# Two of three short DFTs on TensorE with 64-row tiles instead of 32-row tiles

## The chip, the cores and the metric

One core of one Trainium2 chip. The metric is the device time of one execution in microseconds (us). Executions of one kernel differ by up to about 1 us here, so medians are quoted, and every timed kernel was run in turn with the kernel before on the same chip. A ratio below is the mean time of one kernel's runs over that of the other's of the same rounds, so it is not quite the ratio of the medians.

TensorE is written PE, VectorE DVE, ScalarE ACT, GpSimd POOL, as the profile does. PEld is PE's weight loads. "Granted clock" is the share of PE's full clock that the profile records: 0.50 or 1.00 in the fast runs here.

## The reference, cut to what matters

```python
P = jnp.exp(logdA[:, :, None] * l[None, None, :])
K = jnp.einsum("dn,dnl,dn->dl", Cc, P, dB).real      # one kernel K per channel d
Kf = rfft(pad(K)); Uf = rfft(pad(u))
y  = irfft(Uf * Kf)[:L]                              # long convolution
h  = x + y + u * Dskip
out = h + SwiGLU(layernorm(h))
```

There are 640 channels and 2048 tokens. Only the transform of K (`Kf` above) is changed. The kernel works on blocks of 256 tokens, so the transform of K is a DFT over 256 positions, l = 16 j + i, and it is done in three chunks of 256, 256 and 128 channels.

## The kernel before: the parts that matter

`k_mm` leaves K in PSUM with 128 partitions that are 4 pairs of channels x 16 values of j x 2 channels of the pair. `k_evac` copies it to SBUF as `kc` and multiplies with a mask that keeps the row's own channel of the pair. `k_dft` contracts over the partitions with the DFT table `wt`, in four 32-row tiles, each into a part of PSUM of its own. Their matmuls overlap in the trace: in chunk 2 one starts every 8.1 ns, and each is shown as about 0.19 us long. For each of 16 values of i and 4 parts f of the output there are 4 loads and 4 matmuls: 256 of each per chunk.

```python
def k_evac(h, pk, kc, b):
    ...
    for c2 in range(2):
        src = pk[...].rearrange("p h (g x c) -> p x h g c", g=gh, c=2)[:, :, :, :, c2]
        dst = ...
        S.mul(out=dst, in_=src, mul=mask[:, c2:c2 + 1])      # 128 x 512

def k_dft(h, kc, mid=None):
    cg, nu = CHUNKS[h] // 8, 4 // CUT[h]
    pp = [ps2("g"), ps2("g")]
    for i in range(II):                                       # 16
        if mid and i == II // 2:
            mid()
        for f in range(NFT):                                  # 4
            for blk in range(4):
                T.matmul(pp[blk // 2][:, blk % 2, f * 2 * cg:(f + 1) * 2 * cg],
                         lhsT=wt[32 * blk:32 * blk + 32, i, f * P:(f + 1) * P],
                         rhs=kc[32 * blk:32 * blk + 32, (i * nu + blk % nu) * 2 * cg: ...],
                         ..., tile_position=(32 * blk, 0))
    return pp
```

`rhs` has 64 columns in chunks 0 and 1 and 32 in chunk 2. `kf_evac` then copies the result into `kf` on ScalarE, and the convolution's product (`z`, line 586) reads `kf` on VectorE. The stretch of the schedule around chunk 2 that the argument turns on, in program order:

```python
for b in range(n_mm(2)):
    k_evac(2, k_mm(2, at2, bt2, b), kc, b)
run(p0, 1)
stats(1)                                   # 1/sqrt(var): 3 steps on DVE, 8 on POOL
kr_mul(SPLIT[0], (0,))                     # ACT
inv(0, SPLIT[0])                           # PE, ACT
ln1(1)                                     # DVE: normalise, needs stats(1)
h_add(0, SPLIT[0], (0,))                   # DVE
pb = k_dft(2, kc, lambda: [fwd(0, SPLIT[1], part) for part in range(2)])
kr_mul(SPLIT[0], (1,))                     # ACT
kf_evac(2, pb, "SSSS")                     # ACT, copies of kf
...
run(p0)                                    # DVE: product with kf of chunk 2
```

Of the kernel before, what the change touches and what calls it, by code (L numbers as in the profile page):

```python
# [8 lines left out]
F32 = mybir.dt.float32  # L9
I32 = mybir.dt.int32  # L10
ACT = mybir.ActivationFunctionType
ALU = mybir.AluOpType

TB = 256
NFT = 4
JJ = 16
II = 16
EPS = 1e-5
CHUNKS = [256, 256, 128]
CUT = [4, 2, 2]  # L20
# [3 lines left out]
def mkap(t, offset, dims):  # L24
    return bass.AP(tensor=t.tensor, offset=t.offset + offset, ap=[list(d) for d in dims])

@with_exitstack
def kernel(
    ctx: ExitStack,
    tc: tile.TileContext, A_u, A_A_re, A_A_im, A_B_re, A_B_im,  # L30
         A_C_re, A_C_im, A_log_dt, A_Dskip, B_x, B_w1, B_w3, B_w2, out, dbg=None):
    nc = tc.nc
    P = nc.NUM_PARTITIONS
# [9 lines left out]
    V, S, T, G = nc.vector, nc.scalar, nc.tensor, nc.gpsimd  # L43
    CWM = 3 * max(CHUNKS) // 2
    d0s = [sum(CHUNKS[:h]) for h in range(len(CHUNKS))]
# [3 lines left out]
    def ps2(tag="d", dt=F32):  # L49
        return ps.tile([P, 2, 512 if dt == F32 else 1024], dt, name="ps2", tag=tag, bufs=2)  # L50

    dram = ctx.enter_context(tc.tile_pool(name="dram", bufs=1, space=bass.MemoryType.DRAM))
    keep = ctx.enter_context(tc.tile_pool(name="keep", bufs=1, side="left"))
# [4 lines left out]
    early = ectx.enter_context(tc.tile_pool(name="early", bufs=1, side="right"))  # L58
# [38 lines left out]
    toki = early.tile([P, 2], I32, name="toki")  # L97
# [7 lines left out]
    V.tensor_copy(out=tokf[:], in_=toki[:])  # L105
    parity = early.tile([P, 1], I32, name="parity")
    V.tensor_single_scalar(out=parity[:], in_=toki[:, 0:1], scalar=1, op=ALU.bitwise_and)
    mask = keep.tile([P, 2], F32, name="mask")
    sil = keep.tile([P, 1], F32, name="sil")
    V.tensor_scalar(out=mask[:, 0:1], in0=parity[:], scalar1=-1.0 / TB, scalar2=1.0 / TB, op0=ALU.mult, op1=ALU.add)  # L110
    V.tensor_scalar(out=mask[:, 1:2], in0=parity[:], scalar1=1.0 / TB, scalar2=None, op0=ALU.mult)
    angs = []

    def angle(kt):
# [19 lines left out]
    wt = kp.tile([P, II, NFT * P], BF16, name="wt")  # L134
# [177 lines left out]
    def k_mm(h, at, bt, b):  # L312
        nt, cg = CUT[h], CHUNKS[h] // 8
        gw, gh = 3 * cg // 2, min(4 * nt, cg // 2)
        m, n = P // nt, 8 // nt
        pk = ps2()

        def mm(half, gi, part, n1, first, last):
            g = (cg + gh * b + gi) if n1 else (half * (cg // 2) + gh * b + gi)
            r = slice(64 * half, 64 * half + 64) if n1 else slice(0, P)  # L320
            for t in range(nt):
                c = (part * gw + g) * P
                T.matmul(pk[m * t:m * t + m, half, gi * m:gi * m + m].rearrange("p (i c) -> p i c", c=n),  # L323
                         lhsT=at[r, c + m * t:c + m * t + m],
                         rhs=bt[r, c:c + P].rearrange("p (i m) -> p i m", m=8)[:, :, n * t:n * t + n],
                         start=first, stop=last, tile_position=(r.start, m * t), skip_group_check=True)

        for half in range(2):
            for gi in range(gh):
                for part in range(2):  # L330
                    mm(half, gi, part, False, gi == 0 and part == 0, False)
        for gi in range(gh):
            for part in range(2):
                for half in range(2):
                    mm(half, gi, part, True, False, gi == gh - 1 and part == 1)
        return pk
# [4 lines left out]
    def k_evac(h, pk, kc, b):  # L341
        nt, cg = CUT[h], CHUNKS[h] // 8
        gh, nu = min(4 * nt, cg // 2), 4 // nt
        for c2 in range(2):
            src = pk[:, :, 0:P // nt * gh].rearrange("p h (g x c) -> p x h g c", g=gh, c=2)[:, :, :, :, c2]
            dst = mkap(kc[:], c2 + 2 * gh * b, [[kc[:].ap[0][0], P], [2 * cg, II * nu], [cg, 2], [2, gh]])
            S.mul(out=dst, in_=src, mul=mask[:, c2:c2 + 1])  # L347

    def k_dft(h, kc, mid=None):
        cg, nu = CHUNKS[h] // 8, 4 // CUT[h]  # L350
        pp = [ps2("g"), ps2("g")]
        for i in range(II):
            if mid and i == II // 2:
                mid()
            for f in range(NFT):
                for blk in range(4):
                    T.matmul(pp[blk // 2][:, blk % 2, f * 2 * cg:(f + 1) * 2 * cg], lhsT=wt[32 * blk:32 * blk + 32, i, f * P:(f + 1) * P],  # L357
                             rhs=kc[32 * blk:32 * blk + 32, (i * nu + blk % nu) * 2 * cg:(i * nu + blk % nu + 1) * 2 * cg], start=(i == 0 and f == 0), stop=(i == II - 1 and f == NFT - 1),
                             tile_position=(32 * blk, 0), skip_group_check=True)
        return pp  # L360

    def kf_evac(h, pp, engs):
        cg, d0 = CHUNKS[h] // 8, d0s[h]
        for k in range(2):
            for f2 in range(2):
                src = pp[k][:, :, 0:NFT * 2 * cg].rearrange("p b (f g c) -> p f g b c", f=NFT, c=2)[:, 2 * f2:2 * f2 + 2]
                dst = mkap(kf[:], f2 * 2 * D + d0 + 4 * k, [[kf[:].ap[0][0], P], [D, 2], [8, cg], [2, 2], [1, 2]])
                if engs[2 * k + f2] == "S":
                    S.copy(out=dst, in_=src)
                else:  # L370
                    V.tensor_copy(out=dst, in_=src)
# [157 lines left out]
    kc = kp.tile([P, II * 4 * (max(CHUNKS) // 8)], BF16, name="kc", bufs=1)  # L529
    pk = k_mm(0, at0, bt0, 0)  # L530
    stg = [b_rest(1, bt1, "sin", ig) for ig in IGS]
    k_evac(0, pk, kc, 0)
    at2 = kp.tile([P, 2 * JJ * CWM], BF16, name="at", bufs=1)
    S.copy(out=a_view(2, at2)[:, :, :, 0, :], in_=wl2[:].rearrange("p a (q c) -> p a q c", c=2))
    z_mul(1, zs1, ze1)
    run(a_chain(1, at1, zs1))
    pb = k_dft(0, kc)
    for ig, st in zip(IGS, stg):
        b_mul(1, bt1, "sin", ig, st)
    zs2 = z_sin(2)  # L540
    bt2 = b_tile(2)
    b_first(2, bt2, "sin", 1, 8)
    kf_evac(0, pb, "SSSS")
    b_first(2, bt2, "sin", 8, II)
    for k in range(2):
# [9 lines left out]
    kc = kp.tile([P, II * 4 * (max(CHUNKS) // 8)], BF16, name="kc", bufs=1)  # L555
    for b in range(n_mm(1)):
        k_evac(1, k_mm(1, at1, bt1, b), kc, b)
        if b == 0:
            sums(1, 0)
# [5 lines left out]
    for ig, st in zip(IGS, stg):  # L565
        b_mul(2, bt2, "exp", ig, st)
    pb = k_dft(1, kc)
    for part in range(2):
        fwd(0, SPLIT[0], part)
    kf_evac(1, pb, "SSSS")  # L570
    skip(0, ulns[0])
    kc = kp.tile([P, II * 4 * (max(CHUNKS) // 8)], BF16, name="kc", bufs=1)
# [60 lines left out]
    def kr_mul(r, parts=(0, 1)):  # L633
        for part in parts:
            for e in range(2):
                S.mul(out=kr[:, part, e, r], in_=kf[:, 1 - part, e, r], mul=(1.0 if part == e else -1.0))
# [5 lines left out]
    for b in range(n_mm(2)):  # L642
        k_evac(2, k_mm(2, at2, bt2, b), kc, b)
# [4 lines left out]
    ln1(1)  # L648
    h_add(0, SPLIT[0], (0,))
    pb = k_dft(2, kc, lambda: [fwd(0, SPLIT[1], part) for part in range(2)])  # L650
    kr_mul(SPLIT[0], (1,))
    kf_evac(2, pb, "SSSS")
    kctx.close()
    if dbg and "kf" in dbg:
# [76 lines left out]
    for part in range(2):  # L731
        fwd(1, HALVES[1], part)
    kr_mul(SPLIT[1])
    S.activation(out=sil[:], in_=mask[:, 0:1], func=ACT.Silu)
    idle = xs[:, 12:14, 0:256].rearrange("p a (b c) -> p a b c", b=1)
    warm(7, idle)
    h_add(0, SPLIT[1])
# [111 lines left out]
```

## Time and profile before

| | |
|---|---|
| median, 20 runs | 293.88 us (293.34 to 294.40) |
| the profiled run | 294.6 us, span 292.6 us |
| first gate/up matmul of SwiGLU | 112.2 us |
| from there to the end | 180.35 us, PE almost without a break |

The span has two halves. After about 112 us PE works without a break on SwiGLU; before, ACT and DVE are the busy engines and PE waits. So a change in the K-DFT can help only by letting the first gate/up matmul start earlier.

The chain of waits of the kernel before, from 96 to 113 us (start in us, duration in us, what), shows where that start comes from:

```profile
96.59 1.05 PE ps_2186 L604 x2
97.64 0.14 PE ps_2205 L357 x2
...
98.46 0.34 issue
98.81 0.20 PE ps_2205 L357
...
100.30 1.05 ACT kr L636 x2
101.35 2.07 issue
103.42 0.61 ACT kf L369 x3
104.04 0.02 issue
104.06 0.43 DVE z L586
```

L357 is the K-DFT of chunk 2. "issue" is time for which the profile shows nothing that was waited for; the one of 2.07 us stands before the copies of kf, which wait for the K-DFT. The timeline of PE's loads in that K-DFT (start us, duration us, engine, line, operation, shape, count, and in brackets the idle time before) shows what PE did meanwhile:

```profile
97.56 0.80 PEld L357 LDWEIGHTS <-wt 32*128 32x128 bf16 x89 [0.84 <-issue]
98.80 0.38 PEld L357 LDWEIGHTS <-wt 32*128 32x128 bf16 x39 [0.44 <-issue]
99.76 0.76 PEld L357 LDWEIGHTS <-wt 32*128 32x128 bf16 x85 [0.20 <-issue]
102.80 0.41 PEld L357 LDWEIGHTS <-wt 32*128 32x128 bf16 x43 [2.28 <-issue]
```

PE loaded 89 tables and stopped, then 39 and 85 (the transform `mid` sits between), and stopped again for over 2 us, with operands ready (the last copy into `kc` ended at 97.32 us) and 43 pairs of load and matmul to go. From the first gap to the second there are 39 + 85 such pairs and the 8 instructions of `mid`: 2 x 124 + 8 = 256 instructions. The trace has 11 stops of this kind, and from one to the next lie 254 to 256 recorded loads and matmuls, once 512 (3351 loads and 3349 matmuls are recorded, so a few records are missing). On VectorE the stop is a wait of 1.18 us (timeline of DVE, same columns):

```profile
102.19 0.69 DVE L622 BATCH_NORM_STATS2 hst<-xs 128x6 f32<-128x512 bf16 x1
104.06 0.43 DVE L586 TENSOR_TENSOR z<-vt,kf 128x512 bf16<-128x512 bf16 x1 [1.18 <-ACT kf L369]
```

And the queue that fetches instructions, from the page's list of DMA queues (packets, MB, share of 16 engines' span):

```profile
q8 instruction: 26, 0.43, 0.6%
```

0.43 MB in 26 packets is 16 KB each. The 6700 recorded loads and matmuls of PE make 258 per packet, so I take a packet for a block of 256 PE instructions, 64 bytes each (an estimate from these counts).

### The profile page before, as it was taken

What the parts mean: (1) busy time and instruction counts of PE and PEld (TensorE: products, weight loads), DVE (VectorE), ACT (ScalarE), POOL (GpSimd) and SP (SyncE); (2) the same over time, 40 slices, a digit from 0 to 9 for tenths busy, and PEclk for the clock granted to TensorE, in tenths of its full rate; (3) what the DMA queues carried; (4) which work ended last, traced back from release to release, by engine and by line L of the source; (5) the groups of instructions that cost most, each with busy time, mean ns of one, the idle gap of its engine ahead of it and who ended that gap; (6) DMA issues with size and microseconds to landing.
All of it is one profiled execution on the core that took longest, in us unless ns stands there. A gap on an engine that the chain in (4) does not pass through costs nothing.

```text
span 292.6 us, 8071 instructions
## 1 busy us (share of the span) xinstructions
PE 230.3 (79%) x3349; PEld 181.2 (62%) x3351; DVE 230.0 (79%) x512; ACT 210.7 (72%) x450; POOL 53.0 (18%) x171
## 2 busy tenths in 40 slices
PE   3541174234854689999999999999999999999995
PEld 1320133131743437867887887887887887887883
DVE  6799999999899678979949949949959958932111
ACT  3999999999988678867676677677574574553440
POOL 4000100000422203536322322322320020020000
PEclk9999987557565559999999999999999999999999
DMA  5741840000000059800000000000000000000001
GB/s 150 230 204 39 188 99 4 4 2 1 4 4 3 6 165 348 298 1 25 24 2 24 25 0 25 22 2 22 26 0 25 24 2 22 25 0 25 22 2 46
DMA packets 12166, 15.65 MB, mean 53 GB/s; under 512 B 2018, under 2 KB 11490, under 8 KB 12002
## 3 DMA queue, kind: packets, MB, share of 16 engines
q1 hardware_dynamic: 11570, 14.95, 16.7%
q8 instruction: 26, 0.43, 0.6%
q10 hardware_dynamic: 560, 0.20, 0.3%
q14 instruction: 10, 0.08, 0.1%
HBM read 12.26 MB, written 2.88 MB: 52 GB/s over the span
## 4 chain that ended last, share of the span: by engine, by line
PE 59%; ACT 25%; DVE 11%; issue 2%; DMA 1%; POOL 0%; DVEq 0%; ACTq 0%
ACT bt L251 5%; ACT bt L248 3%; ACT stg L245 2%; ACT stg L248 2%; ACT bt L245 2%; PE ps_2941 L709 1%; ACT zs L211 1%; ACT ze L219 1%; PE ps_5107 L709 1%; PE ps_5077 L709 1%; PE ps_4890 L709 1%; PE ps_3967 L709 1%; PE ps_3894 L709 1%; PE ps_3625 L709 1%; PE ps_4296 L709 1%
## 5 line engine op out<-in xcount | busy, mean ns | idle before, releaser
L695 PEld LDWEIGHTS <-w1sb 128*128 128x128 bf16 x480 | 46.9, 98 | 8.2 <-issue 0.7
L695 PEld LDWEIGHTS <-w3sb 128*128 128x128 bf16 x480 | 47.0, 98 | 5.4
L703 DVE TENSOR_TENSOR hm<-sg,up 128x512 bf16<-128x512 bf16 x48 | 19.7, 420 | 34.1 <-ACT up L702 34.1
L709 PEld LDWEIGHTS <-hm 128*128 128x128 bf16 x384 | 37.3, 98 | 14.0 <-issue 0.4
L423 ACT ACTIVATE jk<-xs 128x640 bf16<-128x640 bf16 x32 | 23.8, 744 | 0.6
L405 POOL TENSOR_TENSOR ta<-rs 128x2 f32<-128x2 f32 x30 | 8.6, 287 | 78.9 <-DVE rs L403 77.7
L323 PEld LDWEIGHTS <-at 128*32 128x32 bf16 (+3 forms) x896 | 12.8, 121 | 14.9 <-issue 11.6
L304 DVE TENSOR_TENSOR at<-at,zs 128x1536 bf16<-128x1536 bf16 (+3 forms) x30 | 20.4, 679 | 0.0
L306 DVE TENSOR_TENSOR tt<-at,zs 128x1536 bf16<-128x1536 bf16 (+3 forms) x30 | 20.2, 675 | 0.0
L309 DVE TENSOR_TENSOR at<-at,tt 128x1536 bf16<-128x1536 bf16 (+3 forms) x30 | 19.1, 679 | 0.5
L357 PEld LDWEIGHTS <-wt 32*128 32x128 bf16 x768 | 8.9, 111 | 16.6 <-issue 16.6
L430 POOL TENSOR_SCALAR mv<-sm 128x2 f32<-128x2 f32 x8 | 4.3, 542 | 67.7 <-ACT jk L423 67.7
L377 PEld LDWEIGHTS <-ident 128*128 128x128 bf16 x41 | 5.1, 131 | 17.8 <-DVE at L309 7.5
L622 DVE BATCH_NORM_STATS2 hst<-xs 128x6 f32<-128x320 bf16 (+2 forms) x32 | 14.3, 486 | 0.5
L723 DVE TENSOR_TENSOR ot<-ob,xs 128x640 bf16<-128x640 bf16 x15 | 7.3, 487 | 7.5 <-ACT ob L722 7.5
L591 DVE TENSOR_TENSOR xf<-z 128x1280 bf16<-128x1280 bf16 x14 | 11.6, 825 | 0.8
L357 PE MATMUL ps_1065<-kc,wt 32*128 32x64 bf16 x128 | 3.5, 230 | 8.9 <-ACT kc L347 7.6
L323 PE MATMUL ps_477<-bt,at 128*32 128x32 bf16 (+1 forms) x512 | 4.9, 196 | 6.9 <-issue 6.9
L237 POOL MEMSET bt<- 128x384 bf16 (+1 forms) x3 | 1.1, 364 | 50.4 <-PE ps_477 L323 25.2
L412 POOL TENSOR_TENSOR rs<-rs,ta 128x2 f32<-128x2 f32 x30 | 9.6, 319 | 2.5
L279 DVE TENSOR_TENSOR bt<-bt,stg 128x1920 bf16<-128x1920 bf16 (+1 forms) x9 | 8.9, 989 | 0.3
L377 PE MATMUL ps_424<-at,ident 128*128 128x256 bf16 x14 | 3.2, 419 | 7.3 <-DVE at L309 7.3
(533 smaller groups left out, 660.9 us busy)
## 6 DMA issues: line engine op xcount, KB each, us to landing
xs<-in_A_u_dram SPq DMA_DIRECT2D x4, 640.0 KB, 5.5
out_dram<-ot SPq DMA_DIRECT2D x15, 160.0 KB, 1.8
wt<-ftd SPq DMA_DIRECT2D x4, 512.0 KB, 7.6
w1sb<-in_B_w_dram SPq DMA_DIRECT2D x3, 640.0 KB, 6.9
w3sb<-in_B_w_dram SPq DMA_DIRECT2D x3, 640.0 KB, 8.2
w2sb<-in_B_w_dram SPq DMA_DIRECT2D x1, 1920.0 KB, 14.7
ftd<-fl SPq DMA_DIRECT2D x1, 256.0 KB, 2.2
par_ar<-in_A_A_re_dram SPq DMA_DIRECT2D x2, 96.0 KB, 2.5
```

What stands on the lines that cost most here:

```text
L248: S.activation(out=dst, in_=grp(h, 1), func=ACT.Sin, scale=float(i), bias=math.pi / 2)
L251: S.activation(out=dst, in_=grp(h, 1), func=ACT.Sin, scale=-float(i))
L304: V.tensor_tensor(out=av[:, part, :, o0:o0 + w, :], in0=src, in1=z4[:, 0].broadcast_to([P, cw // 2, w, 2]), op=ALU.mult)
L306: V.tensor_tensor(out=tv[:, part], in0=src, in1=z4[:, 1].broadcast_to([P, cw // 2, w, 2]), op=ALU.mult)
L309: V.tensor_tensor(out=dst, in0=dst, in1=tv[:, 1 - part], op=(ALU.add if part else ALU.subtract))
L323: T.matmul(pk[m * t:m * t + m, half, gi * m:gi * m + m].rearrange("p (i c) -> p i c", c=n), lhsT=at[r, c + m * t:c + m * t + m], rhs=bt[r, ...
L357: T.matmul(pp[blk // 2][:, blk % 2, f * 2 * cg:(f + 1) * 2 * cg], lhsT=wt[32 * blk:32 * blk + 32, i, f * P:(f + 1) * P], rhs=kc[32 * blk:3 ...
L423: S.activation(out=jk[:], in_=xs[:, 2 * c + k, :], func=f, accum_out=st1[c][:, m, k:k + 1])
L622: V.bn_stats(out=st[:, k, int(r.start > 0), :], in_=xs[:, 2 * c + k, r])
L695: T.matmul(pg[:, b, u * TB:(u + 1) * TB], lhsT=w[:, kt, fb * P:(fb + 1) * P], rhs=xts[c][:, kt, :], start=(kt == 0), stop=(kt == DT - 1))
L703: V.tensor_tensor(out=hms[c][:, 2 * fp:2 * fp + 2, :].rearrange("p u t -> p (u t)"), in0=sg[:], in1=up[:], op=ALU.mult)
L709: T.matmul(po[:, q, 0:D // 2], lhsT=hms[c][:, fb, k * P:(k + 1) * P], rhs=w2sb[:, fb, q * (D // 2):(q + 1) * (D // 2)], start=(fb == 0), s ...
```

## The change

The intent, as I read it: half as many, twice as large PE instructions in the K-DFT of chunks 1 and 2. A 64-row tile takes two 32-row blocks at once. Its columns are then the channels of both blocks, so K must be zero wherever a row meets a column of the other block; the mask gets a second form for that, and `k_evac` writes each half separately. Chunk 0 is left as it is.

```diff
-    mask = keep.tile([P, 2], F32, name="mask")
+    mask = keep.tile([P, 3, 2], F32, name="mask")
 ...
+    V.tensor_scalar(out=half[:], in0=toki[:, 0:1], scalar1=5, scalar2=1, op0=ALU.arith_shift_right, op1=ALU.bitwise_and)
+    V.tensor_copy(out=halff[:], in_=half[:])
+    V.tensor_scalar(out=mask[:, 2, :], in0=mask[:, 0, :], scalar1=halff[:], scalar2=None, op0=ALU.mult)
+    V.tensor_tensor(out=mask[:, 1, :], in0=mask[:, 0, :], in1=mask[:, 2, :], op=ALU.subtract)
 ...   (k_evac)
-        for c2 in range(2):
-            S.mul(out=dst, in_=src, mul=mask[:, c2:c2 + 1])
+        for u in range(nu):
+            for c2 in range(2):
+                S.mul(out=dst, in_=src, mul=mask[:, (1 + u if nu == 2 else 0), c2:c2 + 1])
 ...   (k_dft)
-                for blk in range(4):
-                    T.matmul(... lhsT=wt[32 * blk:32 * blk + 32, i, f * P:(f + 1) * P],
-                             rhs=kc[32 * blk:32 * blk + 32, <2*cg columns>], tile_position=(32 * blk, 0), ...)
+                for t in range(nt):                  # nt = 2 in chunks 1 and 2
+                    T.matmul(... lhsT=wt[m * t:m * t + m, i, f * P:(f + 1) * P],
+                             rhs=kc[m * t:m * t + m, i * n:(i + 1) * n], tile_position=(m * t, 0), ...)   # n = 4*cg
```

Per chunk that is 128 loads and 128 matmuls instead of 256 and 256, with 128 columns instead of 64 in chunk 1 and 64 instead of 32 in chunk 2. `kf_evac` reads the new layout with the same four copies.

More of the change, by code (lines that the diff above doesn't have):

```diff
@@ L107 @@
     V.tensor_single_scalar(out=parity[:], in_=toki[:, 0:1], scalar=1, op=ALU.bitwise_and)
-    mask = keep.tile([P, 2], F32, name="mask")
+    mask = keep.tile([P, 3, 2], F32, name="mask")
     sil = keep.tile([P, 1], F32, name="sil")
-    V.tensor_scalar(out=mask[:, 0:1], in0=parity[:], scalar1=-1.0 / TB, scalar2=1.0 / TB, op0=ALU.mult, op1=ALU.add)
-    V.tensor_scalar(out=mask[:, 1:2], in0=parity[:], scalar1=1.0 / TB, scalar2=None, op0=ALU.mult)
+    V.tensor_scalar(out=mask[:, 0, 0:1], in0=parity[:], scalar1=-1.0 / TB, scalar2=1.0 / TB, op0=ALU.mult, op1=ALU.add)
+    V.tensor_scalar(out=mask[:, 0, 1:2], in0=parity[:], scalar1=1.0 / TB, scalar2=None, op0=ALU.mult)
+    half = early.tile([P, 1], I32, name="half")
+    V.tensor_scalar(out=half[:], in0=toki[:, 0:1], scalar1=5, scalar2=1, op0=ALU.arith_shift_right, op1=ALU.bitwise_and)
+    halff = early.tile([P, 1], F32, name="halff")
+    V.tensor_copy(out=halff[:], in_=half[:])
+    V.tensor_scalar(out=mask[:, 2, :], in0=mask[:, 0, :], scalar1=halff[:], scalar2=None, op0=ALU.mult)
+    V.tensor_tensor(out=mask[:, 1, :], in0=mask[:, 0, :], in1=mask[:, 2, :], op=ALU.subtract)
     angs = []
@@ L343, in k_evac @@
         gh, nu = min(4 * nt, cg // 2), 4 // nt
-        for c2 in range(2):
-            src = pk[:, :, 0:P // nt * gh].rearrange("p h (g x c) -> p x h g c", g=gh, c=2)[:, :, :, :, c2]
-            dst = mkap(kc[:], c2 + 2 * gh * b, [[kc[:].ap[0][0], P], [2 * cg, II * nu], [cg, 2], [2, gh]])
-            S.mul(out=dst, in_=src, mul=mask[:, c2:c2 + 1])
-    def k_dft(h, kc, mid=None):
-        cg, nu = CHUNKS[h] // 8, 4 // CUT[h]
-        pp = [ps2("g"), ps2("g")]
+        for u in range(nu):
+            for c2 in range(2):
+                src = pk[:, :, 0:P // nt * gh].rearrange("p h (g i u c) -> p i u h g c", g=gh, u=nu, c=2)[:, :, u, :, :, c2]
+                dst = mkap(kc[:], u * 2 * cg + c2 + 2 * gh * b, [[kc[:].ap[0][0], P], [nu * 2 * cg, II], [cg, 2], [2, gh]])
+                S.mul(out=dst, in_=src, mul=mask[:, (1 + u if nu == 2 else 0), c2:c2 + 1])
+    def k_dft(h, kc, mid=None):
+        nt, cg = CUT[h], CHUNKS[h] // 8
+        nu = 4 // nt
+        m, n = P // nt, nu * 2 * cg
+        tiles = [ps2("g") for _ in range(nt // 2)]
+        pp = [tiles[t // 2][:, t % 2, 0:NFT * n] for t in range(nt)]
         for i in range(II):
@@ L355, in k_dft, with kf_evac @@
             for f in range(NFT):
-                for blk in range(4):
-                    T.matmul(pp[blk // 2][:, blk % 2, f * 2 * cg:(f + 1) * 2 * cg], lhsT=wt[32 * blk:32 * blk + 32, i, f * P:(f + 1) * P],
-                             rhs=kc[32 * blk:32 * blk + 32, (i * nu + blk % nu) * 2 * cg:(i * nu + blk % nu + 1) * 2 * cg], start=(i == 0 and f == 0), stop=(i == II - 1 and f == NFT - 1),
-                             tile_position=(32 * blk, 0), skip_group_check=True)
-        return pp
-    def kf_evac(h, pp, engs):
-        cg, d0 = CHUNKS[h] // 8, d0s[h]
+                for t in range(nt):
+                    T.matmul(pp[t][:, f * n:(f + 1) * n], lhsT=wt[m * t:m * t + m, i, f * P:(f + 1) * P],
+                             rhs=kc[m * t:m * t + m, i * n:(i + 1) * n], start=(i == 0 and f == 0), stop=(i == II - 1 and f == NFT - 1),
+                             tile_position=(m * t, 0), skip_group_check=True)
+        return tiles
+    def kf_evac(h, tiles, engs):
+        cg, d0, nt = CHUNKS[h] // 8, d0s[h], CUT[h]
+        nu = 4 // nt
         for k in range(2):
             for f2 in range(2):
-                src = pp[k][:, :, 0:NFT * 2 * cg].rearrange("p b (f g c) -> p f g b c", f=NFT, c=2)[:, 2 * f2:2 * f2 + 2]
+                if nu == 1:
+                    src = tiles[k][:, :, 0:NFT * 2 * cg].rearrange("p b (f g c) -> p f g b c", f=NFT, c=2)
+                else:
+                    src = tiles[0][:, k, 0:NFT * 4 * cg].rearrange("p (f b g c) -> p f g b c", f=NFT, b=2, c=2)
+                src = src[:, 2 * f2:2 * f2 + 2]
                 dst = mkap(kf[:], f2 * 2 * D + d0 + 4 * k, [[kf[:].ap[0][0], P], [D, 2], [8, cg], [2, 2], [1, 2]])
@@ L733 @@
     kr_mul(SPLIT[1])
-    S.activation(out=sil[:], in_=mask[:, 0:1], func=ACT.Silu)
+    S.activation(out=sil[:], in_=mask[:, 0, 0:1], func=ACT.Silu)
     idle = xs[:, 12:14, 0:256].rearrange("p a (b c) -> p a b c", b=1)
```

## The prediction

> **What bounds the kernel now.** The chain of waits splits the run. From about 126 us to 289 us it is almost pure TensorE (20-matmul groups of 2.18 us, 24-matmul groups of 3.26 us, full clock); the change touches none of that. Before it, ScalarE and VectorE carry the chain: DVE is busy without a break from 70 to 96.6 us (windows view). The chain passes through the K-DFT in only one place: chunk 2. There DVE finishes its statistics at 102.9 us and then idles 1.18 us until ScalarE's copies of kf, which wait for the last K-DFT matmuls (timeline).
>
> **Why that K-DFT is late.** The matmuls of chunk 2 run from 97.57 to about 103.3 us, but PE issues nothing at 98.46-98.81 and again for 2.17 us, 100.63-102.80. These "issue" gaps return every 256 PE instructions; each ends 2.3 to 2.9 us after a 16 KB packet of the instruction queue starts. [...] a dense stream gets one block per 3.5 to 4 us. Each K-DFT is 512 PE instructions, two blocks.
>
> **What the change does.**
> - Removes 128 loads and 128 matmuls from each of chunks 1 and 2: exactly one block each, so later block boundaries keep their phase.
> - Doubles the columns: chunk 1 goes from 64 groups of four 32-row tiles x 64 columns to 64 pairs of 64-row tiles x 128; chunk 2 from 32 to 64 columns. At the half clock granted here (0.50) the trace shows 53 ns per group of 64 columns, so I estimate 107 ns per pair in chunk 1 and 53 ns in chunk 2.
> - Chunk 1: 81.64-87.16 us before, including a 1.56 us gap. Estimate after: 64 pairs, part at full clock, 5 to 5.7 us without that gap. No gain, and none needed: the next matmul waits for usd (87.08) anyway and the copies of kf come at 91.5.
> - Chunk 2: 64 x 53 ns = 3.4 us plus 0.5 us for the transform in its middle. The first 87 load-matmul pairs finish the block at about 100.4, when the next block (due 98.8) is there; the rest fits into it. End about 101 to 101.8 instead of 103.3.
> - k_evac: 2 ACT copies of 128x512 (0.67 us apart) become 4 of 128x256, about 0.38 us each (estimate): +0.2 us per call, three calls; all but the last have slack, the last shifts the start of K-DFT 2 by 0 to 0.1 us.
> - Four tiny DVE instructions at the start, about 0.7 us (dependent ones step 0.2 us), inside an idle of 0.80 us before dtb: cost about 0 to 0.1 us.
>
> **On the critical path.** kf of chunk 2 can be ready near 102.2; DVE is free at 102.9 instead of starting at 104.06. Gain at most 1.18 us; the later chain (inverse, statistics, transposes, first gate/up matmul at 112.2, and the weight DMAs released by kf at 104.2) shifts with it. Predicted 292.8 us, range 291.9 to 293.9. Chances: faster by over 2% 0.01, within 2% 0.98, slower 0.01.
>
> **What would show it.** 24 packets of the instruction queue; no issue gap over 1 us inside either K-DFT; DVE's wait for kf near zero; first gate/up matmul near 111.1; the tail from there unchanged at about 177 us.
>
> **What would make it wrong.** 64-row loads that don't hide under the other tile's matmul; a fetch that still stalls K-DFT 2; its start delayed by ScalarE; another granted clock in 97-112 us; start-up DVE work delaying the first exponentials.

The sum: of the wait of 1.18 us about 1.1 us gained, 293.88 to 292.8 us.

## The result, and the profile after

293.32 us (median of 10 runs, 293.11 to 293.61) against 293.88 us (20 runs). The ratio is 0.9984, 95% interval 0.9975 to 0.9992: a gain of about 0.5 us, clear of noise and far under 2%. Executions over 1.5% slower than the fastest of the same kernel are left out of the means. All outputs are right.

The profiled runs differ by more, 292.6 against 291.4 us of span. All of it comes before the first gate/up matmul (112.21 us before, 111.02 us after); from there to the end it is 180.35 us in both. (The 177 us of the prediction fit the end of the last matmul, at 289.0 us before, and not the end of the span.)

The chain of waits of the changed kernel in the same stretch:

```profile
99.25 0.81 DVE uln L475 x2
...
101.68 0.70 DVE xs L631
102.41 0.69 DVE hst L637
103.10 0.32 DVE z L601
```

The chain no longer passes through the K-DFT (line 367 now) at all: it stays on DVE. PE's loads in the K-DFT of chunk 2 after the change run in one piece on each side of `mid`:

```profile
97.51 1.73 PEld L367 LDWEIGHTS <-wt 64*128 64x128 bf16 x64 [0.83 <-issue]
99.88 1.02 PEld L367 LDWEIGHTS <-wt 64*128 64x128 bf16 x64 [0.20 <-issue]
```

The last of its matmuls starts at 100.83 us instead of 103.13. On the timeline of DVE the wait for kf is gone, and `z` starts at the end of the instruction before it:

```profile
102.41 0.69 DVE L637 BATCH_NORM_STATS2 hst<-xs 128x6 f32<-128x512 bf16 x1
103.02 0.41 DVE L601 TENSOR_TENSOR z<-vt,kf 128x512 bf16<-128x512 bf16 x1
```

Two blocks fewer are fetched:

```profile
q8 instruction: 24, 0.39, 0.6%
```

DVE, however, is later here: its statistics end at 103.10 us, against 102.88 before. That delay starts in the first microseconds. The start of the timeline of DVE before:

```profile
2.11 0.61 DVE L117 TENSOR_SCALAR ang<-oddf,tokf 128x256 int32<-128x256 int32 x2
2.76 0.51 DVE L119 TENSOR_SCALAR ang<-ang 128x512 int32<-128x512 int32 x1
4.06 0.39 DVE L163 CAST dtf<-dtb 128x2 f32<-128x2 bf16 x1 [0.80 <-ACT dtb L160]
4.14 0.32 DVE L164 TENSOR_SCALAR dtf<-dtb 128x2 f32<-128x2 bf16 x1
4.49 0.74 DVE L167 TENSOR_SCALAR dg<-ident,dtf 128x128 bf16<-128x128 bf16 x4
```

and after:

```profile
2.11 0.14 DVE L113 TENSOR_SCALAR half<-toki 128x1 int32<-128x1 int32 x1
...
2.83 0.16 DVE L117 TENSOR_TENSOR mask<-mask 128x2 f32<-128x2 f32 x1
2.90 1.08 DVE L123 TENSOR_SCALAR ang<-oddf,tokf 128x256 int32<-128x256 int32 x2
4.02 0.60 DVE L125 TENSOR_SCALAR ang<-ang 128x512 int32<-128x512 int32 x1
4.55 0.15 DVE L169 CAST dtf<-dtb 128x2 f32<-128x2 bf16 x1
```

The four mask instructions move the first `ang` from 2.11 to 2.90 us, which the wait of 0.80 us would have held. But the two `ang` now take 1.08 us instead of 0.61, so `dtf` starts at 4.55 instead of 4.06. ScalarE's first copy of the parameters, from which all exponentials follow, starts at 6.77 us instead of 6.54. Why the two `ang` took longer was not tested.

So two things had to be explained: whether the missing stall is really due to the number of PE instructions, and why the median gained only about half of what the two profiles show.

### The profile page after: what moved, and what is told of

Read it like the earlier page. It is cut to its first block, busy times and chain, and to the rows that moved or that the text cites. A ratio compares the mean times of both kernels' runs of the same rounds, so it can differ in the third digit from the quotient of the medians.

```text
span 291.4 us, 7569 instructions
## 1 busy us (share of the span) xinstructions
PE 226.7 (78%) x3093; PEld 180.4 (62%) x3095; DVE 230.9 (79%) x516; ACT 211.2 (72%) x456; POOL 53.3 (18%) x171
## 4 chain that ended last, share of the span: by engine, by line
PE 57%; ACT 24%; DVE 11%; DMA 4%; issue 1%; POOL 1%; DVEq 0%; ACTq 0%; POOLq 0%
ACT bt L257 5%; DMA w2sb<-in_B_w_dram 4%; ACT bt L254 3%; ACT stg L251 2%; ACT stg L254 2%; ACT bt L251 2%; PE ps_2695 L724 1%; ACT zs L217 1%; ACT ze L225 1%; PE ps_4861 L724 1%; PE ps_4831 L724 1%; PE ps_3990 L724 1%; PE ps_3721 L724 1%; PE ps_3037 L724 1%; PE ps_2964 L724 1%
## 5 line engine op out<-in xcount | busy, mean ns | idle before, releaser
L329 PEld LDWEIGHTS <-at 128*32 128x32 bf16 (+3 forms) x896 | 10.6, 109 | 14.5 <-issue 11.4
L367 PEld LDWEIGHTS <-wt 32*128 32x128 bf16 (+1 forms) x512 | 11.3, 117 | 12.0 <-issue 11.9
L619 PEld LDWEIGHTS <-gt 128*128 128x128 bf16 x48 | 4.5, 98 | 7.0 <-DVE z L603 5.6
```

The costliest lines, as they stand in the source:

```text
L329: T.matmul(pk[m * t:m * t + m, half, gi * m:gi * m + m].rearrange("p (i c) -> p i c", c=n), lhsT=at[r, c + m * t:c + m * t + m], rhs=bt[r, ...
L367: T.matmul(pp[t][:, f * n:(f + 1) * n], lhsT=wt[m * t:m * t + m, i, f * P:(f + 1) * P], rhs=kc[m * t:m * t + m, i * n:(i + 1) * n], start= ...
```

## The experiments

Theory 1: the gain comes from fewer PE instructions. K-DFT 2 of the kernel before uses up 256 instructions in 1.8 us (98.80 to 100.63 us), while two packets of the instruction queue start 3.7 us apart there (96.19 and 99.92 us in the trace file); with half as many instructions, K-DFT 2 would not have to wait for a packet. Rivals: the wider tiles themselves are faster; or the higher clock (the granted clock in 100 to 101 us was 0.50 in the profile before and 1.00 after); or chunk 1 gives the gain.

### The kernel before against itself

No edit.

> The kernel before, unchanged, against itself: the ratio should be 1.000, and its interval is the resolution. It also gives a second profile of the kernel before. The profiled run of before took 294.6 us, 0.7 above its median, and its three blocks of PE instructions before and in K-DFT 2 took 1.37 to 1.43 us to fetch, where most others took 0.93 to 0.96. Theory A (fetch times of single runs explain why the profile lost 1.2 us and the median 0.56): a profiled run near 293.9 has K-DFT 2 end 0.5 to 1 us earlier than 103.3, with shorter fetches. Theory B (the granted clock of single runs explains it): the fetches are the same, and the stretches at full clock before 110 us differ from run to run.

Measured: ratio 1.0002 (0.9988 to 1.0016). So a batch of this size can't tell a difference of less than about 0.4 us from none. The profiled run took 293.82 us, close to the median. The start and end of its stall (timeline of PE):

```profile
100.12 0.52 PE L357 MATMUL ps<-kc,wt 32*128 32x32 bf16 x41
...
102.28 0.52 PE L357 MATMUL ps<-kc,wt 32*128 32x32 bf16 x43 [1.63 <-issue]
```

and VectorE's wait:

```profile
103.53 0.43 DVE L586 TENSOR_TENSOR z<-vt,kf 128x512 bf16<-128x512 bf16 x1 [0.62 <-ACT kf L369]
```

The stall was 1.63 us instead of 2.18 and the wait 0.62 instead of 1.18. In both profiles the fetch of the block began at about the same time, 99.92 and 99.93 us, but its packet took 1.43 us in the first profile and 0.93 us in this one (single packets stand in the trace file; the page shows only the sums). The granted clock of this stretch, 97 to 104 us, was 0.50 in both. So theory A of the expectation holds for these two profiles: a fetch 0.50 us shorter, a product 0.53 us earlier, a span 0.6 us shorter. The kernel's first profile was one of its slow-fetching runs, and its wait of 1.18 us was not typical.

### The change in one chunk alone

```diff
 def k_dft(h, kc, mid=None):
+    return (k_dft_wide if h in WIDE else k_dft_narrow)(h, kc, mid)   # likewise k_evac, kf_evac
```

with the wide form for chunk 2 alone, then for chunk 1 alone. Chunk 0 is the same in both forms. The four mask instructions stay in both.

> The 64-row tiles in chunk 2 alone. If the gain comes from the stalls in K-DFT 2 alone: same time as the changed kernel, 293.3 us (ratio 0.998), K-DFT 2 over by about 101, DVE waiting under 0.1 us for kf. If chunk 1 gives a part (an earlier clock rise for instance), the time lies between before and after, and the clock in 86 to 97 us is 0.5.

Measured: 293.48 us (293.27 to 293.51), ratio 0.9987 (0.9974 to 1.0000). The kernel before had a median of 293.66 us in these rounds and the interval touches 1, so the time alone doesn't show a gain here; the profile carries the argument. K-DFT 2 had no stall; its last matmul started at 101.50, the product at 103.06, at the end of DVE's statistics (103.14). The granted clock was 0.50 from 80.6 to 101.1 us in this profile, that is, through nearly all of K-DFT 2. So the stall goes, and the wait with it, without the higher clock.

> The 64-row tiles in chunk 1 alone. If the gain comes from chunk 2: no gain, and a loss of about 0.2 us from the four added mask instructions (ratio 1.000 to 1.001); K-DFT 2 still has its stall over 1 us and ends at 103 or later. If chunk 1's missing stall or the higher clock after it matters: ratio below 0.999.

Measured: 293.74 us (293.48 to 294.33), ratio 0.9998 (0.9984 to 1.0012). A stall of 1.62 us (100.35 to 101.97) stayed in K-DFT 2, though the clock there was 1.00 from 99.4 us. So a full clock did not remove the stall here. The last matmul came at 102.28 us, earlier than the 103 expected, and kf and DVE came free for the product at about the same moment. No gain. The spread is as wide as that of the kernel before, while with chunk 2 changed it is 0.24 us. This fits a time that hangs on a fetch in the one and on DVE in the other.

One thing I had not expected: in `k_mm` of chunk 2, before K-DFT 2, the kernel before has a stall of 1.36 us (93.71 to 95.07), and it is absent from the profiles in which chunk 1 is wide. K's copies for chunk 2 then start at 94.43 instead of 95.81. It bought nothing by itself, as the inverse transform ahead of K-DFT 2 waits for DVE until 96.5 us anyway. What decides when the fetch of a block begins was not settled.

### The masks later

```diff
-    half = ...; halff = ...; mask[:, 2] = ...; mask[:, 1] = ...     # at the start
 ...
     bt0 = b_tile(0)
+    half = ...; halff = ...; mask[:, 2] = ...; mask[:, 1] = ...
     z_mul(0, zs0, ze0)
```

> The changed kernel with the four mask instructions moved behind the first A tile, into a wait of DVE of 0.94 us for ScalarE's sines. In the changed profile the first exponentials' input starts some 0.2 us later than before; if the four instructions cause that, this wins it back: about 293.1 us, 0.2 below the changed kernel, with the DVE product for the diagonal back at 4.5 us. If the shift has another cause (run to run), same time as the changed kernel.

Measured: 293.12 us (292.98 to 293.45), ratio 0.9976 (0.9962 to 0.9989), where the changed kernel had 293.32 and 0.9984. The first copy of the parameters is back at 6.54 us and the product at 102.82 instead of 103.02. So the masks cost 0.2 us, as a difference of medians; the intervals of the ratios overlap, and it is the times in the profiles, equal to those of the kernel before, that carry this: in the table below DVE is free at 103.10 to 103.24 us in the four versions with the masks at the start, and at 102.88 to 102.91 in the kernel before and here. The profiled run, the slowest of the six, lost the 0.2 us again: its clock was 0.50 from 105.9 to 109.4 us, and the ten transposes ahead of the first gate/up matmul took 1.03 us instead of 0.81.

### The number of instructions back, with everything else kept

```diff
-                for t in range(nt):
-                    T.matmul(pp[t][:, f * n:(f + 1) * n], ..., rhs=kc[..., i * n:(i + 1) * n], ...)
+                for q in range(ns):                  # ns = 2 in chunk 2
+                    for t in range(nt):
+                        T.matmul(pp[t][:, f * n + q * w:f * n + (q + 1) * w], ..., rhs=kc[..., i * n + q * w: ...], ...)   # w = n // ns
```

> The changed kernel, but in chunk 2 each 64-column matmul is cut into two of 32 columns with their own load: the same 64-row tiles, the same columns streamed, but 512 PE instructions again as before. Theory 1 (the gain comes from fewer PE instructions to fetch): one stall of 1.2 to 2.2 us returns in K-DFT 2, which then ends at 102.2 to 103.2 instead of 101.0; the first product on kf is 0 to 0.5 us later than in the changed kernel; time 293.5 to 293.8. Rival (the gain comes from the wider tiles or from the higher clock that they bring): no such stall or no loss, K-DFT 2 over by 101.3, time 293.3.

Measured: 293.51 us (293.32 to 294.33), ratio 0.9991 (0.9976 to 1.0005). The stall is back, but 0.83 us long and not the 1.2 to 2.2 us expected, and the last matmul starts at 102.19 us. But the product started at 103.08, where it does in the changed kernel, since DVE is not free before 103.15. So the profile agrees with theory 1 and the time does not tell. It showed that in the changed kernel DVE, not K-DFT 2, comes last, and that K-DFT 2 has about 1 us to spare. To see the instruction count in the time, DVE had to be made faster first.

### VectorE relieved

DVE waits 2.24 us for POOL's steps of 1/sqrt(var) before it normalises at 99 us.

```diff
-        st1[c] = (mv, rstd(mv[:, 0:2, 1], 2, G))
+        st1[c] = (mv, rstd(mv[:, 0:2, 1], 2, V if c == 1 else G))
```

First on the kernel before:

> The kernel before, with the six Newton steps of the second chunk pair's statistics on VectorE instead of GpSimd, which takes most of VectorE's 2.2 us wait before the normalisation at 99.0 (six dependent steps of 0.2 us take its place). If K-DFT 2 is what binds the kernel before at 103 to 104 us: VectorE reaches the product some 1 us earlier but waits the longer for kf (0.6 to 1.2 us becomes 1.6 to 2.2), time within 0.2 us of before. If VectorE binds: 1 us faster.

Measured: 293.50 us (293.00 to 293.79), ratio 0.9983 (0.9970 to 0.9996). In the profile DVE's statistics ended at 101.84 us, 1 us earlier, and it then waited for kf:

```profile
103.51 0.43 DVE L586 TENSOR_TENSOR z<-vt,kf 128x512 bf16<-128x512 bf16 x1 [1.67 <-ACT kf L369]
```

The product starts where it did in the second profile of the kernel before (103.53): in this run K-DFT 2 binds. The median still gained 0.4 us, more than I had expected. I would put this down to runs in which fetches are quick and DVE comes last, but no profile of such a run was taken: the profiled run, 293.79 us, was the slowest of the five.

Then on the changed kernel with late masks:

> The same edit on the version with the late masks. There VectorE arrives last (no wait for kf), so it should now pay: VectorE reaches the product about 1 us earlier, at about 101.8 to 102, just when kf is copied; 292.2 to 292.5 us, ratio 0.995. If something else holds the product at 102.8 (the copies of kf, the clock), 293.0.

Measured: 291.94 us (291.78 to 292.73), ratio 0.9936 (0.9922 to 0.9950), faster than both kernels. On the same chip and in the same rounds, the edit on the kernel before gave 293.50. So with DVE out of the way the change (with its masks moved) is worth 1.56 us, three times what it gave alone.

> The changed kernel, unchanged, on the same chip as the three others: 293.3 us, spread half as wide as that of before (0.5 against 1.0 us), K-DFT 2 over by about 101, no wait for kf.

This was the control of that batch. Measured: ratio 0.9981 (0.9969 to 0.9994), close to the 0.9984 above; four runs lie between 293.27 and 293.56 us, with a median of 293.32. The profiled run (298.29 us, mean granted clock 0.902 against 0.934 to 0.947 in the four) is not used.

### The number of instructions, where it can show

The split matmuls on the version with late masks and DVE's statistics, the version itself again, and a third one with `kr_mul(SPLIT[0], (1,))` moved from before the copies of kf to just before `kr_mul(SPLIT[1])`.

> Late masks and statistics on VectorE (291.94 us before this run), with the 64-column matmuls of chunk 2 cut in two: 512 PE instructions in K-DFT 2 again, same tiles and columns. In the split of the changed kernel the stall came back (0.83 us, last matmul at 102.2 instead of 100.8) but VectorE arrived only at 103.1 and hid it. Here VectorE arrives at 101.8, so the instruction count must now show in the time: theory 1 says a product on kf at 102.8 to 103.3 instead of 102.1, and 0.6 to 1.1 us more, 292.5 to 293.1. If the width of the tiles were what mattered: 291.9.

> Late masks and statistics on VectorE once more, on the same chip as the other two: 291.9 us, ratio 0.994.

Measured: split 293.06 us (292.59 to 293.94), ratio 0.9976 (0.9961 to 0.9991); not split 291.99 us (291.89 to 292.46), ratio 0.9940 (0.9927 to 0.9952). The same tiles, the same columns, twice the instructions: 1.07 us more, as predicted. The loads of the split K-DFT 2:

```profile
97.30 1.78 PEld L364 LDWEIGHTS <-wt 64*128 64x128 bf16 x128 [0.83 <-issue]
99.66 1.14 PEld L364 LDWEIGHTS <-wt 64*128 64x128 bf16 x85 [0.20 <-issue]
101.61 0.61 PEld L364 LDWEIGHTS <-wt 64*128 64x128 bf16 x43 [0.81 <-issue]
```

The stop comes ahead of the last 43 loads, as it does in the kernel before, and DVE waits for it:

```profile
103.04 0.42 DVE L604 TENSOR_TENSOR z<-vt,kf 128x512 bf16<-128x512 bf16 x1 [1.18 <-ACT kf L381]
```

The first profile of the version that is not split:

```profile
97.52 1.73 PEld L361 LDWEIGHTS <-wt 64*128 64x128 bf16 x64 [0.84 <-issue]
99.88 1.10 PEld L361 LDWEIGHTS <-wt 64*128 64x128 bf16 x64 [0.20 <-issue]
...
102.14 0.43 DVE L601 TENSOR_TENSOR z<-vt,kf 128x512 bf16<-128x512 bf16 x1 [0.34 <-ACT kf L378]
```

The clock is no explanation: it rose to 1.00 at 99.7 us in the split run and at 100.2 us in the first run that was not split. The last matmul is 1.24 us later (102.15 against 100.91), although the split K-DFT began 0.22 us earlier. The stop itself is 0.71 us of this; the rest goes with the smaller matmuls, which are twice as many and at full clock come every 13 ns with 32 columns, against 14 ns with 64. So this experiment prices the number of instructions, and the wait for a block is only part of that price.

In the change itself the stops are all of the gain in K-DFT 2, and the wider tiles a small loss. Without its stops the K-DFT 2 of the kernel before is about 2.0 us of matmuls (256, one every 8 ns); in the changed kernel it is about 2.6 us (128, one every 26 ns at half clock and every 14 ns at full). What went away are the stops of 0.34 and 2.17 us. That they are waits for the fetch of a block is read from the traces (the spacing of 256, the packets, the fetch and the stop that were 0.5 us shorter together in the second profile); no run changed the fetch alone.

The second run that was not split bears on the clock once more. There PE had full clock from 87.7 to 104.8 us, the copies of kf started already at 99.73 us, and the product at 101.54, when DVE came free. Its first gate/up matmul was at 109.80 us. In the run with the moved copies (below) PE had half clock until 100.5 us and the copies of kf started at 100.88, over 1 us later, and the first gate/up matmul was at 109.79. Once DVE comes last, a still earlier K-DFT 2 no longer helps.

> Late masks and statistics on VectorE, with ScalarE's two copies into kr (1.05 us, 100.3 to 101.35) moved behind the copies of kf. In the profile of that version the last matmul of K-DFT 2 started at 100.91 and the copies of kf at 101.50, and VectorE waited 0.34 us. If ScalarE's order causes this wait: kf about 0.3 us earlier, 291.6 to 291.7 us. If the matmuls' end does: 291.9; if the moved copies now hold up a later one before the first gate/up matmul: slower than 291.9.

Measured: 291.89 us (291.72 to 291.96), ratio 0.9930 (0.9919 to 0.9942). The copies of kf start 0.23 us after the start of the last matmul of K-DFT 2, and DVE does not wait for them. Against 291.99 us of the same rounds this can't be told from no gain: the intervals overlap, and DVE did not wait in the control's profile either.

### The profiles side by side

| run (us) | first copy of parameters | last matmul of K-DFT 2 starts | copies of kf start | DVE free | product starts | first gate/up matmul |
|---|---|---|---|---|---|---|
| before | 6.54 | 103.13 | 103.42 | 102.88 | 104.06 | 112.21 |
| before again | 6.53 | 102.60 | 102.89 | 102.91 | 103.53 | 111.68 |
| changed | 6.77 | 100.83 | 101.50 | 103.10 | 103.02 | 111.02 |
| chunk 2 only | 6.78 | 101.50 | 101.80 | 103.14 | 103.06 | 111.06 |
| chunk 1 only | 6.78 | 102.28 | 102.58 | 103.24 | 103.21 | 111.44 |
| late masks | 6.54 | 100.54 | 101.35 | 102.90 | 102.82 | 111.03 |
| changed, split | 6.78 | 102.19 | 102.44 | 103.15 | 103.08 | 111.24 |
| before, DVE's statistics | 6.53 | 102.58 | 102.87 | 101.84 | 103.51 | 111.66 |
| late masks, DVE's statistics | 6.31 | 100.91 | 101.50 | 101.80 | 102.14 | 110.15 |
| the same, split | 6.53 | 102.15 | 102.40 | 101.86 | 103.04 | 111.06 |
| late masks, DVE's statistics, again | 6.30 | 98.94 | 99.73 | 101.63 | 101.54 | 109.80 |
| the same, kf first | 6.53 | 100.65 | 100.88 | 101.87 | 101.79 | 109.79 |

"DVE free" is the end of its statistics instruction. The product starts at the later of "DVE free" and about 0.64 us after "copies of kf start"; instructions on one engine overlap by up to 0.1 us. The span after the first gate/up matmul is 180.3 us in every row. The first copy at 6.31 us, in both profiles of one version, is not explained: the last version and the split one open with the same code and have 6.53. DVE is free at 101.86 and 101.87 us in these two, against 101.80 and 101.63.

## Why the prediction was right or wrong

The predicted 292.8 us was 0.5 us too low; the range of 291.9 to 293.9 and "within 2%" held, but that range reaches up to the 293.88 us of the kernel before, so no gain at all would have held it too. The mechanism was right, and two terms of its sum were mis-sized: the gain of 1.1 us that it forecast was twice the 0.56 us measured.

- **"These issue gaps return every 256 PE instructions": right.** 24 blocks instead of 26; no issue gap in either K-DFT of the changed kernel; the stall returns with the instructions alone, and the doubled instructions cost 1.07 us where they can show.
- **Durations of the K-DFTs: right.** Chunk 2 was said to end at 101 to 101.8, and its last matmul starts at 100.83. Chunk 1 ran from 82.71 to 88.09 us, 5.4 us, for an estimate of 5 to 5.7. At half clock the matmuls of chunk 1 came every 53 ns, 107 ns per pair, as estimated; those of chunk 2 every 26 ns. The clock rose at 100.0 us, which I had not counted on; with half clock nearly to the end, in the run with chunk 2 alone, the last matmul came at 101.50.
- **"Then idles 1.18 us": the first step that failed.** It was read from one profile, of a run 0.7 us above the median, and was taken for the typical wait. The second profile, at 293.82 us, has 0.62 us. The packets of instruction fetches took 0.93 to 1.43 us in these two profiles, and between the two the wait moved with them. I had the profiled run's time and the median side by side and did not use the difference.
- **"Four tiny DVE instructions ... cost about 0 to 0.1 us": the second step that failed.** The wait of 0.80 us was there and the four instructions took 0.79 us of it, but the two `ang` behind them went from 0.61 to 1.08 us. The cost is 0.2 us (first copy of the parameters 6.54 to 6.77 us; late masks 0.2 us faster).
- **The sum, corrected.** If the second profile is typical, the median run had a wait of about 0.6 us to lose, and the masks take 0.2 us of that. The product moved from 103.53 in the second profile before to 103.02 after, 0.51 us, and the medians moved 0.56 us. The first profile's 1.19 us at the first gate/up matmul is 1.04 us at the product and 0.15 us behind it, where PE's clock was higher after the change (1.00 from 100.0 us on, against 0.50 until 110.3 us before). So it is partly luck that the profile's first gate/up matmul, at 111.02 us, met the 111.1 of the prediction: the higher clock, not counted on, made up for most of what the masks cost.
- **"All but the last have slack" (ScalarE's four copies): right.** They were 0.2 us longer per call (1.72 us for four in place of 1.51 for two in chunk 1; the estimate of 0.38 us is what other copies of 128x256, those to `vt` at 99.65 and 99.92 us, take in the profile before: 0.37 and 0.38 us), and K-DFT 2 started at 97.52 against 97.57, after the inverse transform.
- **"Later block boundaries keep their phase": right, but I missed** that the stall in `k_mm` of chunk 2 would go too. It had no effect on the time.
- **"DVE is busy without a break from 70 to 96.6 us": not exact.** The windows view has DVE busy for 1.28 of the 2 us from 76 to 78; it waits 0.61 us for POOL there. Nothing else in the prediction rests on it.

## What to carry to other kernels

A stop of PE that names no releaser, and returned every 256 instructions, was read here as a sign that instructions arrived more slowly than PE used them up (in K-DFT 2, 256 in 1.8 us against packets 3.7 us apart); fewer, larger matmuls helped there even though they stream twice the columns and half of what they stream is zeros. Before pricing a wait, ask whether the profiled run is typical: here its wait was twice that of a second profiled run, near the median. And when a change takes an engine off the critical path, look at once for what now comes last: the change alone gave 0.5 us, and with the statistics' eight GpSimd steps done as six on VectorE, and four other instructions moved into a wait, it gave 1.9 us (291.9 us).

## What the traces show of instruction fetches and small matmuls

- In the profiles of the kernel before and of the changed one PE stopped 11 and 6 times with no releaser named, for 0.34 to 2.50 us, each stop 256 instructions or a multiple of that after the one before (254 to 256 recorded, or 512). The first instruction after a stop came 2.3 to 2.9 us after the start of a packet of 16 KB, and no two packets started less than 3.4 us apart.
- How far into one block PE must be before the fetch of the next begins was not settled. After 14 of these 17 stops the next packet started 1.0 to 1.6 us after PE went on; after the other three it started 5.7 and 6.4 us after in the kernel before, and 6.5 us after in the changed one. In the two of the kernel before, PE had been held up by waits and long matmuls when it was 68 and 60 instructions into the block, and the fetch began 1.1 and 1.0 us after it went on. No run here settles why.
- In the K-DFT of chunk 2 the four 32-row tiles of the kernel before started a matmul every 8.1 ns at half clock, 32 ns per tile, and the two 64-row tiles of the changed kernel every 14 ns at full clock, 28 to 29 ns per tile.
